# Frequencies to tokens on TensorE: the stationary operand takes all 128 channels in place of 64

## The chip, the cores and the metric

The kernel runs on one core of a Trainium2 chip. The metric is device time in microseconds (us) of one execution. TensorE (PE in the profile) multiplies: a load (PEld) puts the stationary operand into its array, a matmul streams the moving operand past it into a PSUM bank. VectorE (DVE), ScalarE (ACT) and GpSimdE (POOL) do elementwise work, and SyncE (SP) issues the DMA transfers.

## The reference

Two sequences of 3008 tokens with 256 channels are convolved with a filter through a Fourier transform over the tokens, and the tokens go through two multilayer perceptrons one after the other.

```python
def _attn_ref(x, filt_r, filt_i) -> np.ndarray:
    X = np.fft.rfft(x, axis=1)
    F = (filt_r + 1j * filt_i)[None, :, :]
    y = np.fft.irfft(X * F, n=x.shape[1], axis=1)
    return y.astype(np.float32)

def _moe_ref(x, w_gate, w_val, w_out):
    g = x @ w_gate
    silu = g * (1.0 / (1.0 + np.exp(-g)))
    return (silu * (x @ w_val) @ w_out).astype(np.float32)

def _moe2_ref(x, w_in, w_out):
    h = x @ w_in
    relu6 = np.clip(h + 3.0, 0.0, 6.0)
    return ((h * relu6 / 6.0) @ w_out).astype(np.float32)
```

The hidden widths are 1536 and 2048; the weights come in as 64-bit floats, which the kernel decodes itself.

## The kernel before

The transform over 3008 = 47 x 64 points is done as a transform over 47 and one over 64, both as matmuls with small matrices of sines and cosines that lie in the tile `mat`. Going forward, `over_n1` (L335) and `over_n2` (L351) make 24 x 64 frequencies, `filter_product` multiplies by the filter, and `back` (L377) undoes the transform over 64. The result goes to DRAM (`d2`) with the 24 frequencies, real and imaginary, in 48 rows. What is left is the transform back over 47 points: 48 rows of frequencies become 47 tokens. That is **`to_time`** (L157), the function that is changed.

`to_time` works in *turns*. One turn takes the frequencies `g[..., t - t0]` of 128 channels as the stationary operand and up to 47 columns of `mat` as the moving one, so that the 128 channels come out on the partitions of a PSUM bank and the tokens along its columns. A turn is done for r = 0 (rows 0 to 47 of the tiles, bank `accs[0]`) and for r = 1 (rows 64 to 111, bank `accs[1]`): these use the upper and the lower half of the rows of TensorE's array. Before, the 128 channels are also cut into two halves of 64 (`o` = 0 and 64), each with its own half of the array's columns: four matmuls a turn on the four quarters of the array. All operands are full f32.

It is called in three places:

- `form(0)`, at the end of the transform's loop (k = 16), and `form(1)`, in the first step (t = 0) of the first perceptron: 12 turns each, half of them for channels 0 to 127 (a = 0), half for 128 to 255 (a = 1). `form_end` splits the result into a high and a low part (L122 on ACT, L115 on DVE) as the operand `xs` of the perceptron's matmuls (L236, L244).
- `block_to_time`, twice (a = 0 and 1) for each of the token blocks 1 to 5: at t = 19 and 20 for block 1, and by `turn_x` at the place `T` of a unit for blocks 2 to 5. `evacuate` (L545 on ACT, L546 on DVE) copies the two banks away.

Blocks have 1024 tokens, two halves of 512; 512 columns are 12 turns (the first and the last turn are narrower), and the last block of 896 tokens has 10. So there are 12 + 12 + 2 x (4 x 12 + 10) = 140 turns, 560 matmuls before.

After the transform the program is a list of *units*, each one slice of 128 (first perceptron) or 256 (second) hidden columns for one block, written out by hand in the order in which every engine takes it: matmuls of L661 and L706 with f32r operands, 128x128 stationary and up to 512 moving columns. The planner `plan_x` puts `turn_x` for the next block two and one places ahead of its first use.

Of the kernel before, what the change touches and what calls it, by code (L numbers as in the profile page):

```python
# [16 lines left out]
P = 128  # L17
B, S, D = 2, 3008, 256
N1, N2 = 47, 64
N1P = 48  # L20
# [36 lines left out]
M1, CO, SI, NS, FIN, NM = 0, 48, 112, 176, 240, 288  # L57
# [20 lines left out]
def fft_conv_glu_mlp(ctx: ExitStack, tc: tile.TileContext, x, filt, mats, sgn, w1, w2, out):  # L78
    nc = tc.nc
# [9 lines left out]
    mat = keep.tile([P, NM], F32, name="mat")  # L89
# [35 lines left out]
    def rows(i, n=64):  # L125

        return slice(i * 64, i * 64 + n)
# [4 lines left out]
    def turns(first, n):  # L132

        return 32 * first // N1, -(-(32 * first + n // 2) // N1)
# [14 lines left out]
    def to_time(g, first, n, accs, a, at=0):  # L149

        t0, t1 = turns(first, n)
        lo, hi = 32 * first, 32 * first + n // 2
        for t in range(t0, t1):
            i0, i1 = max(lo, t * N1), min(hi, (t + 1) * N1)
            for o in range(0, P, 64):
                for r in range(2):
                    nc.tensor.matmul(accs[r][o:o + 64, at + i0 - lo:at + i1 - lo],  # L157
                                     g[rows(r, N1P), t - t0, o:o + 64],
                                     mat[rows(r, N1P), FIN + i0 - t * N1:FIN + i1 - t * N1])

    def block_to_time(g, block, accs, a):
        t, at = 0, 0
        for _, first, n in block:
            t0, t1 = turns(first, n * N2)
            to_time(g[:, t:t + t1 - t0], first, n * N2, accs, a, at)
            t, at = t + t1 - t0, at + n * N2 // 2
# [103 lines left out]
    with tc.manual_schedule():  # L270
# [176 lines left out]
        def form(j):  # L447
            if j == 0:
                xsd["both"] = new_xs()
            xsd[j] = xsd["both"][:, j * 2048:(j + 1) * 2048].rearrange("p (v k n) -> p v k n", v=2, k=2)  # L450
            accs = [bank("a"), bank("a")]
            for a in range(2):
                to_time(gt[j][a], FIRST[j][0], 512, accs, a, 256 * a)
            return accs
# [112 lines left out]
        for t in range(2 * plain):  # L567
# [55 lines left out]
            if 10 < t < 23:  # L623
                q, r = divmod(t - 11, 2)
# [351 lines left out]
```

## Time and profile before

| | |
|---|---|
| median of 3 runs | 1122.61 us (1122.2 to 1125.9) |
| the profiled execution: time | 1122.33 us |
| its span from first to last instruction | 1120.3 us |
| granted clock of TensorE, mean | 1.0 |
| busy share: matmuls, weight loads | 99%, 83% |
| busy share: DVE, ACT, POOL | 76%, 67%, 54% |

Matmuls are pipelined and overlap, so the busy share of the matmuls says that some matmul was in the array, not how fast they follow each other. For that, one reads how far apart the starts of loads or matmuls lie. A record's own duration is longer than that distance. In the views below a run of equal instructions is one row: its start, the time from the first start to the last end, and how many there are. Shapes such as `48*64 48x47` read: stationary operand of 48 rows and 64 columns, moving operand of 48 rows and 47 columns.

### The profile page before, as it was taken

Reading aid. Unit: us, or ns where it says so; the run is one execution under the profiler, and the core shown is the slowest. Engines: PE = TensorE matmul, PEld = TensorE weight load, DVE = VectorE, ACT = ScalarE, POOL = GpSimd, SP = SyncE. Lnnn points to the kernel's source line nnn. Section 1 sums busy time; section 2 is a strip of 40 time slices with the busy share of each in tenths; the row PEclk is TensorE's granted clock in tenths of the full one; section 3 lists DMA queues with packets and bytes.
Section 4 is the critical chain, followed back from the end, with each engine's and each line's share of the span. In section 5 each row is a group of like instructions: output and inputs, shape, how many; then the busy total and the mean of one; then the engine's idle time right before and its main releaser. Section 6 shows DMA issues by size and latency. Waiting matters only on the chain.

```text
span 1120.3 us, 19185 instructions
## 1 busy us (share of the span) xinstructions
PE 1109.2 (99%) x7246; PEld 924.5 (83%) x7246; DVE 856.1 (76%) x1164; ACT 751.8 (67%) x1363; POOL 605.0 (54%) x779
## 2 busy tenths in 40 slices
PE   9989999999999999999999999999999999999998
PEld 7768888888888888888899888888888888888997
DVE  4979977878878887786888877667677677677765
ACT  4554546667667767766767777777777677677764
POOL 4742366696765585574577645335435444354440
PEclk9999999999999999999999999999999999999999
DMA  9974954843733463272353421422322312412300
GB/s 315 284 204 144 265 203 144 233 154 122 196 124 121 141 177 104 83 202 80 116 199 125 165 82 70 153 77 65 142 78 78 138 68 78 148 52 77 116 27 33
DMA packets 58844, 150.75 MB, mean 135 GB/s; under 512 B 5568, under 2 KB 26016, under 8 KB 56992
## 3 DMA queue, kind: packets, MB, share of 16 engines
q1 hardware_dynamic: 58208, 149.01, 41.7%
q8 instruction: 56, 0.92, 0.3%
q10 hardware_dynamic: 544, 0.52, 0.1%
q14 instruction: 36, 0.29, 0.1%
HBM read 117.27 MB, written 32.24 MB: 133 GB/s over the span
## 4 chain that ended last, share of the span: by engine, by line
PE 95%; DVE 2%; POOL 1%; DMA 1%; ACT 1%; issue 0%; ACTq 0%; POOLq 0%; DVEq 0%
PE gv L661 45%; PE a L706 37%; PE gv L236 5%; PE a L244 2%; PE gv L377 1%; PE a L351 1%; PE gv L157 1%; PE gv L335 1%; POOL h L115 1%; DVE h L364 0%; DMA ring<-x_in 0%; DVE xs L115 0%; POOL h L118 0%; DMA w1f<-x 0%; DVE h L600 0%
## 5 line engine op out<-in xcount | busy, mean ns | idle before, releaser
L661 PE MATMUL gv<-xs,wu 128*128 128x512 f32 (+1 forms) x2268 | 566.8, 386 | 0.6 <-DVE h L600 0.6
L115 POOL TENSOR_TENSOR wu<-st,wu 128x224 fp32r<-128x224 f32 x432 | 312.7, 756 | 394.5 <-ACT wu L516 394.5
L661 PEld LDWEIGHTS gv<-xs,wu 128*128 128x128 f32 x2268 | 423.7, 188 | 81.6 <-ACT raw L545 1.7
L706 PE MATMUL a<-hs,wo 128*128 128x512 f32 (+1 forms) x1872 | 476.7, 385 | 0.0
L706 PEld LDWEIGHTS a<-hs,wo 128*128 128x128 f32 x1872 | 351.4, 188 | 65.4 <-ACT hs L694 0.3
L115 DVE TENSOR_TENSOR hs<-h,hs 128x512 fp32r<-128x512 f32 (+3 forms) x228 | 234.6, 1029 | 67.4 <-ACT hs L694 62.8
L694 ACT CAST hs<-h 128x512 fp32r<-128x512 f32 (+3 forms) x216 | 172.6, 799 | 126.7 <-DVE h L690 73.9
L115 POOL TENSOR_TENSOR wo<-st,wo 128x256 fp32r<-128x256 f32 x156 | 149.8, 973 | 0.0
L690 DVE SCALAR_TENSOR_TENSOR h<-h,gv 128x512 f32<-128x512 f32 (+1 forms) x144 | 96.5, 670 | 22.8 <-ACT h L684 22.6
L516 ACT CAST wu<-st 128x384 fp32r<-128x384 f32 x216 | 110.6, 563 | 0.4 <-DMA st<-w1f 0.4
L682 ACT ACTIVATE h<-gv 128x512 f32<-128x512 f32 (+1 forms) x120 | 70.7, 589 | 59.2 <-PE gv L661 57.8
L118 DVE TENSOR_TENSOR gv<-gv,h 128x512 f32<-128x512 f32 (+1 forms) x108 | 74.0, 685 | 41.9 <-PE gv L661 35.3
L684 ACT ACTIVATE h<-gv 128x512 f32<-128x512 f32 (+1 forms) x144 | 84.1, 584 | 15.4 <-PE gv L661 15.3
L871 ACT COPY gv<-gv 128x512 f32<-128x512 f32 (+1 forms) x108 | 60.9, 564 | 42.4 <-PE gv L661 38.6
L118 DVE TENSOR_TENSOR h<-gv,h 128x512 f32<-128x512 f32 (+1 forms) x108 | 73.0, 676 | 18.7 <-PE gv L661 18.3
L690 DVE SCALAR_TENSOR_TENSOR h<-h,h 128x512 f32<-128x512 f32 (+1 forms) x48 | 32.7, 681 | 58.7 <-ACT h L684 58.6
L875 ACT COPY h<-gv 128x512 f32<-128x512 f32 (+1 forms) x108 | 62.5, 579 | 16.4 <-PE gv L661 13.3
L688 DVE TENSOR_TENSOR h<-h 128x512 f32<-128x512 f32 (+1 forms) x60 | 61.6, 1027 | 1.8 <-ACT h L682 1.2
L115 DVE TENSOR_TENSOR xs<-raw,xs 128x512 fp32r<-128x512 f32 (+1 forms) x77 | 57.4, 747 | 0.1
L516 ACT CAST wo<-st 128x256 fp32r<-128x256 f32 (+1 forms) x108 | 54.1, 501 | 0.0
L559 ACT CAST xs<-raw 128x512 fp32r<-128x512 f32 (+1 forms) x77 | 45.7, 609 | 3.0 <-DVE raw L115 2.8
L236 PE MATMUL gv<-xs,wall_a 128*128 128x512 f32 x192 | 45.8, 392 | 0.1
(88 smaller groups left out, 898.1 us busy)
## 6 DMA issues: line engine op xcount, KB each, us to landing
st<-w1f SPq DMA_DIRECT2D x60, 576.0 KB, 3.9
st<-w2f SPq DMA_DIRECT2D x48, 704.0 KB, 4.2
raw<-w_in SPq DMA_DIRECT2D x16, 512.0 KB, 4.6
ring<-x_in SPq DMA_DIRECT2D x30, 256.0 KB, 5.3
x<-w_in SPq DMA_DIRECT2D x9, 768.0 KB, 5.3
d<-turned SPq DMA_DIRECT2D x32, 192.0 KB, 5.2
yd<-y SPq DMA_DIRECT2D x5, 1024.0 KB, 6.6
raw<-yd SPq DMA_DIRECT2D x5, 1024.0 KB, 7.1
```

Of the source, the lines that this page charges most:

```text
L115: (engine or nc.vector).tensor_tensor(out=out, in0=a, in1=b, op=ALU.subtract)
L118: (engine or nc.vector).tensor_tensor(out=out, in0=a, in1=b, op=ALU.add)
L236: nc.tensor.matmul(acc, w[:, r, c[k]:c[k] + P], xs[:, v, k], start=(r, v, k) == (0, 0, 0), stop=(r, k) == (1, 1))
L516: nc.scalar.copy(out=to[:, 0, at:at + hi - lo], in_=src[:, lo:hi])
L661: nc.tensor.matmul(acc[:, :n], w[:, r, FORM[a] * P:(FORM[a] + 1) * P], xs_part(k, v, i), start=start and q == 0, stop=q == 2, skip_group_c ...
L682: nc.scalar.activation(out=self.value(t, 0), in_=src, func=AF.Silu)
L684: nc.scalar.activation(out=self.value(t, a), in_=src, func=AF.Relu, bias=3.0)
L688: nc.vector.tensor_tensor(out=self.value(t, 0), in0=self.value(t, 0), in1=src, op=ALU.mult)
L690: nc.vector.scalar_tensor_tensor(out=self.value(t, a), in0=self.value(t, a), scalar=6.0, in1=src, op0=ALU.min, op1=ALU.mult)
L694: nc.scalar.copy(out=self.hs[:, t, :, 0, :self.n], in_=self.value(t))
L706: yield lambda t=t, v=v, a=a, j=j, r=r: nc.tensor.matmul(banks["a"][2 * j + t][:, :n], self.wo[:, r, (2 * a + j) * P:(2 * a + j + 1) * P], ...
L875: nc.scalar.copy(out=u.s7, in_=b3[:, :n])
```

## The change

The loop over the two halves of the channels goes, and the stationary operand of a matmul takes all 128 channels. A turn then has two matmuls, one on the upper and one on the lower half of the array's rows, each over all of its columns, instead of four. What is multiplied and where it is written stay the same.

```diff
             i0, i1 = max(lo, t * N1), min(hi, (t + 1) * N1)
-            for o in range(0, P, 64):
-                for r in range(2):
-                    nc.tensor.matmul(accs[r][o:o + 64, at + i0 - lo:at + i1 - lo],
-                                     g[rows(r, N1P), t - t0, o:o + 64],
-                                     mat[rows(r, N1P), FIN + i0 - t * N1:FIN + i1 - t * N1])
+            for r in range(2):
+                nc.tensor.matmul(accs[r][:, at + i0 - lo:at + i1 - lo], g[rows(r, N1P), t - t0],
+                                 mat[rows(r, N1P), FIN + i0 - t * N1:FIN + i1 - t * N1])
```

On TensorE, at the start of a burst for the third block (in the middle of the units; `gv0` and `gv1` are its two banks, and a row gives the partitions and columns that are written), the first two turns stand so before:

```order
L706 MATMUL a3_114<-hs_2641,wo_2526 128x512
L157 MATMUL gv0_107<-mat_69,g_2369 64x10
L157 MATMUL gv1_108<-mat_69,g_2369 64x10
L157 MATMUL gv0_107<-mat_69,g_2369 64x10
L157 MATMUL gv1_108<-mat_69,g_2369 64x10
L157 MATMUL gv0_107<-mat_69,g_2369 64x47
L157 MATMUL gv1_108<-mat_69,g_2369 64x47
L157 MATMUL gv0_107<-mat_69,g_2369 64x47
L157 MATMUL gv1_108<-mat_69,g_2369 64x47
```

and so in the changed kernel, whose lines have lower numbers by one here and by two further down:

```order
L704 MATMUL a3_114<-hs_2545,wo_2430 128x512
L156 MATMUL gv0_107<-mat_69,g_2273 128x10
L156 MATMUL gv1_108<-mat_69,g_2273 128x10
L156 MATMUL gv0_107<-mat_69,g_2273 128x47
L156 MATMUL gv1_108<-mat_69,g_2273 128x47
```

The two matmuls on channels 64 to 127 of each turn are gone, and the ones that stay write 128 partitions. Nothing else moves: the instruction ahead of the burst is the same.

The other place is where `form(0)` ends and `back(15)` begins, on TensorE too, between the transform and the first perceptron. Before, the last turn (21 columns) and the first matmuls behind it, which also work on quarters of the array, are these:

```order
L157 MATMUL a0_111<-mat_69,g_1016 64x21
L157 MATMUL a1_112<-mat_69,g_1016 64x21
L157 MATMUL a0_111<-mat_69,g_1016 64x21
L157 MATMUL a1_112<-mat_69,g_1016 64x21
L377 MATMUL gv3_110<-h_1234,mat_69 64x384
L377 MATMUL gv0_107<-h_1234,mat_69 64x384
```

In the changed kernel:

```order
L156 MATMUL a0_111<-mat_69,g_1016 128x47
L156 MATMUL a1_112<-mat_69,g_1016 128x47
L156 MATMUL a0_111<-mat_69,g_1016 128x21
L156 MATMUL a1_112<-mat_69,g_1016 128x21
L375 MATMUL gv3_110<-h_1234,mat_69 64x384
L375 MATMUL gv0_107<-h_1234,mat_69 64x384
```

Here the matmuls ahead of `back(15)` now use the array in halves, and those of `back(15)` still in quarters.

## Rows read from the trace of the kernel before

**Rows 1.** The page's first part: busy time, share of the span, instructions.
```profile
span 1120.3 us, 19185 instructions
PE 1109.2 (99%) x7246; PEld 924.5 (83%) x7246; DVE 856.1 (76%) x1164; ACT 751.8 (67%) x1363; POOL 605.0 (54%) x779
```

**Rows 2.** The page's chain that ended last: shares by engine, then by line.
```profile
PE 95%; DVE 2%; POOL 1%; DMA 1%; ACT 1%; issue 0%; ACTq 0%; POOLq 0%; DVEq 0%
PE gv L661 45%; PE a L706 37%; PE gv L236 5%; PE a L244 2%; PE gv L377 1%; PE a L351 1%; PE gv L157 1%; PE gv L335 1%; POOL h L115 1%; DVE h L364 0%; DMA ring<-x_in 0%; DVE xs L115 0%; POOL h L118 0%; DMA w1f<-x 0%; DVE h L600 0%
```

**Rows 3.** Busy time by stretch: length, PE, PEld, DVE, ACT, POOL, clock, DMA.
```profile
84.00:1119.00 1035.00, 1031.54 (x5476) 865.53 (x5474) 796.01 (x1065) 707.42 (x1252) 557.35 (x709) 1.00 0.39 124
```

**Rows 4.** Line L157: durations in ns (least/median/most), first and last start, shapes.
```profile
L157 PEld LDWEIGHTS gv<-mat,g x928: 129/135/135, 154.1 to 519.9; 48*64 48x64 f32 x186
...
L157 PEld LDWEIGHTS a<-mat,g x96: 129/135/136, 68.6 to 73.5; 48*64 48x64 f32 x96
...
L157 PEld LDWEIGHTS a<-mat,y x48: 129/135/135, 78.3 to 78.9; 48*64 48x64 f32 x48
...
L157 PEld LDWEIGHTS a<-mat,turned x48: 135/135/135, 79.0 to 79.6; 48*64 48x64 f32 x48
```

**Rows 5.** Timeline of TensorE's weight loads around two block bursts.
```profile
229.36 1.49 PEld L157 LDWEIGHTS gv<-mat,g 48*64 48x64 f32 x96 [0.35 <-issue]
230.90 0.19 PEld L661 LDWEIGHTS gv<-xs,wu 128*128 128x128 f32 x1
...
509.74 1.26 PEld L157 LDWEIGHTS gv<-mat,g 48*64 48x64 f32 x80 [0.35 <-issue]
```

**Rows 6.** Weight-load timeline, the last loads before a wait in `form(0)`.
```profile
69.98 0.20 PEld L157 LDWEIGHTS a<-mat,g 48*64 48x64 f32 x4
...
70.04 0.14 PEld L157 LDWEIGHTS a<-mat,g 48*64 48x64 f32 x2
```

**Rows 7.** Weight-load timeline of `over_n2`: quarters, 384 moving columns.
```profile
10.77 0.14 PEld L351 LDWEIGHTS a<-g,mat 64*64 64x64 f32 x4 [0.18 <-issue]
11.09 0.14 PEld L351 LDWEIGHTS a<-g,mat 64*64 64x64 f32 x4 [0.18 <-issue]
11.41 0.14 PEld L351 LDWEIGHTS a<-g,mat 64*64 64x64 f32 x4 [0.18 <-issue]
```

**Rows 8.** Loads of 128 columns: line L244, then two behind a burst (timeline).
```profile
L244 PEld LDWEIGHTS a<-hs,wall_b x48: 186/188/189, 155.6 to 183.9; 128*128 128x128 f32 x48
...
155.62 0.30 PEld L244 LDWEIGHTS a<-hs,wall_b 128*128 128x128 f32 x2
```

**Rows 9.** Loads of the opening stretch: groups (mean ns), then their timeline.
```profile
L320 PEld LDWEIGHTS gv<-turned 128*128 128x128 f32 x16 | 3.5, 330 | 1.1 <-DVE turned L314 1.1
L335 PEld LDWEIGHTS gv<-mat,ring 48*64 48x64 f32 x32 | 0.9, 218 | 0.2 <-issue 0.2
...
1.05 3.49 PEld L320 LDWEIGHTS gv<-turned 128*128 128x128 f32 x16 [1.05 <-DVE turned L314]
4.76 0.95 PEld L335 LDWEIGHTS gv<-mat,ring 48*64 48x64 f32 x32 [0.22 <-issue]
```

**Rows 10.** Timeline of TensorE's matmuls from `form(0)` to behind `form(1)`.
```profile
69.46 0.83 PE L157 MATMUL a<-mat,g 48*64 48x47 f32 x40
72.09 0.31 PE L157 MATMUL a<-mat,g 48*64 48x47 f32 x2 [1.80 <-DMA g<-d]
72.90 0.83 PE L157 MATMUL a<-mat,g 48*64 48x47 f32 x43 [0.50 <-DMA g<-d]
...
78.28 0.91 PE L157 MATMUL a<-mat,y 48*64 48x26 f32 x48
79.01 0.89 PE L157 MATMUL a<-mat,turned 48*64 48x26 f32 x48
79.83 4.47 PE L236 MATMUL gv<-xs,wall_a 128*128 128x512 f32 x16
```

**Rows 11.** Weight-load timeline where the perceptron first reads the second half's `xs`.
```profile
83.56 0.76 PEld L236 LDWEIGHTS gv<-xs,wall_a 128*128 128x128 f32 x4 [0.54 <-DVE xs L115]
```

## Prediction

> **What bounds the kernel now.** I first read the page's busy shares: TensorE's matmuls cover 99% of a span of 1120.3 us, and VectorE, the next busiest compute engine, 76% [rows 1]. The chain that ended last says the same more sharply: 95% of it is TensorE, and the changed line, L157, stands in it with 1% [rows 2]. Then I asked by stretch: from 84 us to the end, matmuls are busy in 1031.54 of 1035.00 us, at a granted clock of 1.00 [rows 3]. So whatever the order of the program puts on TensorE between 84 us and the end, longer or shorter, moves the end by as much; the other engines have slack. The change touches TensorE alone, so the question is how long a burst of turns lasts. Here the reader must not go by busy time, but by the distance of starts.
>
> **How a burst is paced now.** Line L157 has 928 + 96 + 48 + 48 = 1120 weight loads of 48x64, each with one matmul [rows 4]. The program has 560 matmuls there, so an f32 matmul goes through the array in two passes, and each pass loads its weights anew. A turn has four matmuls on four quarters; as these run side by side, I count in *rounds*: four loads, one for each quarter, and four matmuls. That makes 1120 / 4 = 280 rounds, two a turn.
>
> A burst of 96 loads (24 rounds) lasts 1.49 us from the first load's start to the last one's end [rows 5]; less the last load's own 0.135 us [rows 4] that is 1.355 us for 23 distances, **59 ns a round**. The burst of 80 gives (1.26 - 0.135) / 19 = 59 ns [rows 5].
>
> What sets the 59 ns? There are three candidates. First, the matmul: with 384 moving columns the rounds on quarters are 0.32 us apart (10.77, 11.09, 11.41) [rows 7], which is 0.83 ns a column; 47 columns would need 39 ns, too little. Second, issuing eight instructions: when the first half of `form(0)` runs out, only two quarters have work left, and the pairs of loads still start at 69.98 and 70.04 [rows 6], 0.06 us apart with half as many instructions. So it isn't the number of instructions. Third, the load of 64 columns. Its price shows in the step from 64 to 128 columns: the records last 135 ns [rows 4] and 188 ns [rows 8], 53 ns for 64 columns more. A round of 59 ns is then a load of 53 ns and some 6 ns around it, with the matmul of 39 ns running beside the next load. This is the reading that I take.
>
> **The change, part by part.** It removes 560 loads and 560 matmul passes, and the 560 loads that stay are of 128 columns. The two halves of the array have their own rows and their own banks, so I take it that they still run side by side. A turn keeps its two rounds; a round now has two loads of 128 columns beside each other. If the load paces, the round becomes 59 + 53 = **112 ns**.
>
> The trace has no 48x128 load with f32, so I bound the step from both sides. Low: where two loads of 128 columns follow each other with nothing between (155.62, two in 0.30 us, less 0.188), they start 0.11 us apart [rows 8]; that gives 110 - 59 = 51 ns a round. High: in the opening stretch everything on TensorE is slower, but the ratio can be read: 16 full-array f32 passes start (3.49 - 0.33) / 15 = 211 ns apart, and 8 rounds on quarters (0.95 - 0.218) / 7 = 105 ns [rows 9]; twice as long for twice the columns, which here would be 118 ns, 59 more. I take 53, which is a difference of two durations of the same kind at the same clock.
>
> The sum:
>
> - *Ten block bursts*, eight of 24 rounds and two of 20: 232 rounds, all in the stretch where TensorE has no slack [rows 3]. 232 x 53 ns = **+12.3 us**. Behind a burst, `evacuate` waits as before; ACT and DVE get the banks later by as much as TensorE goes on later.
> - *`form(1)`*, 24 rounds, lies between matmuls of L236 without a wait of TensorE [rows 10]: **+1.3 us**.
> - *`form(0)`*: its first 12 rounds end ahead of a wait of 1.80 us for the load of `g` [rows 10] and their 0.6 us disappear in it. The other 12 rounds start when the load lands, and `form_end` and the first L236 wait for them: 12 x 53 ns = **+0.6 us**.
> - *A wait that shrinks*: at 83.56 TensorE's loads wait 0.54 us for DVE's low part of the second half [rows 11]. `form(1)` lasting longer delays TensorE's first step more than DVE's queue, which is busy until then with other work, so some of this is given back: between 0 and 0.5, I take **-0.3 us**.
> - *Change between quarters and halves of the array*: between `form(0)` and `back(15)` both were on quarters. A burst that starts behind full-array work shows 0.35 us without a load [rows 5], most of it the last matmul still streaming. I take **+0.1 us**, from a range of 0 to 0.35. At the other 11 bursts the array changes its division before and after as it did.
>
> Together +12.3 + 1.3 + 0.6 - 0.3 + 0.1 = **+14.0 us**. The profiled execution took 1122.33 us (span 1120.3 and 2.0 around it), so its counterpart takes 1136.3; the median of the runs lies 0.3 above the profiled one, which gives **1136.6 us**, 1.2% slower.
>
> The fewer matmul passes give nothing back, because they were not what paced a round; nothing else leans on TensorE's instruction count.
>
> **The rivals.**
>
> *Nothing changes.* The 59 ns could be a fixed price of any pass, whatever it loads and streams. For it: the 39 ns of the matmul do not explain the round, and the 59 ns hold in bursts with different mixes of narrow turns [rows 5]. Against it: two 128-column loads stood 110 ns apart [rows 8]. It decides if a 128-column load on half the array takes under 59 ns. The time would be 1122.6 (0.1 for `back(15)` is below what can be seen). The Trainium skill, TensorEngine Tiling (Array Packing), section Instruction Overhead, has such a rule: a matmul has an overhead of about 60 cycles, so that one moving column takes as long as sixty. By that rule alone the number of stationary columns would not count at all, and the sum would be nothing; the 110 ns between wide loads speak against leaving the load out.
>
> *Faster.* Issue paces a round after all: 8 instructions in 59 ns become 4 in 29.5, and 268 rounds (280 less the 12 hidden) give -7.9 us, 1114.7. The rows with two quarters at work, still 60 ns apart [rows 6], speak against it, and so do the wide loads [rows 8]. It decides only if a wide load takes less than 59 ns and a round has no floor.
>
> *Load and matmul in series.* With two matmuls in flight instead of four, each half could load, then stream: 59 + 53 + 39 = 151 ns a round, +92 ns; 268 x 92 ns = 24.7, with -0.2 for the last two terms 1147.1. Against it: the quarters with 384 columns are paced by the matmul alone [rows 7], so a quarter loads while it streams.
>
> *The halves' loads in series.* If two wide loads could not go side by side, a round would take 2 x 110 = 220 ns, +161 ns; 268 x 161 ns = 43.1, with the same -0.2 1165.5. Against it: four narrow ones do.
>
> **How the numbers follow.** Load-paced 0.77; in series with the matmul 0.06; the halves in series 0.06; nothing 0.06; faster 0.05. The likeliest's own range: low, 51 ns a round on 268 rounds less 0.5, +13.2, 1135.8; high, 59 ns, nothing given back, 0.35 for the change of division and 0.1 more at each of 11 bursts, +17.3, 1139.9. To leave out no more than 2 in 10 the range goes from 1134 (a little under the low end, for the runs' scatter) to 1148, which takes in the load and matmul in series: 0.77 + 0.06 = 0.83. Under 0.3%, 3.4 us, a measurement of this kernel cannot be told from no change: faster 0.05, same 0.06, slower 0.77 + 0.06 + 0.06 = 0.89.
>
> **What the changed profile would show.** 560 loads of 48x128 at L156, each near 188 ns, and block bursts of 48 loads in (23 x 112 + 188) ns = 2.76 us instead of 1.49: this is the step on which all hangs. The pairs of loads start 112 ns apart; at 59 the fixed price is right, near 150 the series, over 200 the halves exclude each other. The share of L157's successor in the chain doubles to some 2 or 3%. The wait at 83.56 is shorter or gone, the wait of 1.80 us in `form(0)` is shorter by 0.6, and no new wait of TensorE for `raw` shows. The prediction is wrong if a round isn't paced by its load, or if a change between halves and whole or quarters costs other than one between quarters and whole: 11 bursts have two each.

## The result and the profile after

The changed kernel takes 1138.6 us (median of four runs, 1134.84 to 1140.79) against 1122.93 for the kernel before on the same chip: a ratio of 1.0136, 95% interval 1.0116 to 1.0156. The forecast of 1136.6 us lies 2.0 below the median and, as a ratio of 1.0125, inside the interval. Executions that took over 1.5% longer than the fastest of their kernel are left out of every median here: one of the kernel before, one of the forms alone, and the profiled one of the changed kernel's repeat.

The page of the changed kernel, first part, and two lines of its chain that ended last:

```profile
span 1135.1 us, 18065 instructions
PE 1125.8 (99%) x6686; PEld 939.2 (83%) x6686; DVE 853.2 (75%) x1164; ACT 752.4 (66%) x1363; POOL 597.4 (53%) x779
...
PE 96%; DMA 1%; SPq 1%; DVE 1%; POOL 0%; ACT 0%; issue 0%; ACTq 0%; POOLq 0%
PE gv L659 45%; PE a L704 37%; PE gv L234 5%; PE a L242 2%; PE gv L156 2%; PE gv L375 1%; PE a L349 1%; PE gv L333 1%; SPq L384 1%; DMA ring<-x_in 0%; PE a L156 0%; DMA d<-turned 0%; DMA g<-d 0%; POOL h L115 0%; SPq L441 0%
```

Beside [rows 1, 2]: 560 loads and 560 matmuls fewer (6686 for 7246), and yet the matmuls' busy time has risen by 16.6 us and the span by 14.8. The other engines have as much work as before. The block bursts (now L156) have gone from 1% to 2% of the chain.

The same bursts as in [rows 5] and the loads' durations, in the timeline of the weight loads and the view of line L156 (durations least/median/most):

```profile
232.54 2.76 PEld L156 LDWEIGHTS gv<-mat,g 48*128 48x128 f32 x48 [0.35 <-issue]
235.34 0.30 PEld L659 LDWEIGHTS gv<-xs,wu 128*128 128x128 f32 x2
...
521.94 2.31 PEld L156 LDWEIGHTS gv<-mat,g 48*128 48x128 f32 x40 [0.35 <-DMA st<-w1f]
...
L156 PEld LDWEIGHTS gv<-mat,g x464: 182/188/188, 155.1 to 534.1; 48*128 48x128 f32 x155
```

A burst of 24 rounds takes 2.76 us where it took 1.49, one of 20 rounds 2.31 where it took 1.26. A round takes (2.76 - 0.188) / 23 = 112 ns instead of 59. The ten block bursts all show this growth, 8 x 1.27 + 2 x 1.05 = 12.3 us.

One thing in this trace stood in no step of the forecast. The stretches of the changed kernel (length; busy time of PE, PEld, DVE, ACT, POOL; granted clock; DMA share and GB/s) and, from the kernel before, the stretch behind its corresponding burst:

```profile
232.50:235.30 2.80, 2.80 (x49) 2.76 (x48) 0.01 (x1) 0.62 (x1) 2.72 (x6) 1.00 0.73 267
236.20:239.60 3.40, 3.40 (x10) 2.63 (x10) 2.16 (x2) 1.77 (x4) 3.40 (x5) 0.50 0.49 150
240.00:244.00 4.00, 4.00 (x20) 3.24 (x19) 2.26 (x3) 1.93 (x5) 3.61 (x6) 1.00 0.28 108
...
72.40:75.80 3.40, 3.40 (x23) 1.38 (x21) 2.55 (x4) 1.09 (x3) 0.00 (x0) 0.50 0.67 273
```
```profile
232.20:235.60 3.40, 3.40 (x16) 2.77 (x15) 1.77 (x3) 1.97 (x4) 3.40 (x5) 1.00 0.43 115
```

Behind the burst of 232.54 the granted clock is 0.50 for 3.4 us, the lower of the two levels (1.2 instead of 2.4 GHz), and so it is behind `form(0)`. The one behind `form(0)` is no part of the change: it also stands in two kernels below whose `form(0)` is the one of before (half of the channels, and 32 columns for half of the channels; their stretches follow), and not in one whose `form(0)` is changed (falling order).

```profile
74.70:78.10 3.40, 3.40 (x19) 1.74 (x11) 2.99 (x4) 1.73 (x4) 0.00 (x0) 0.50 0.69 282
...
74.30:77.70 3.40, 3.40 (x35) 1.79 (x28) 2.38 (x4) 1.44 (x3) 0.00 (x0) 0.50 0.79 311
```

In the 3.4 us behind the burst 10 matmuls touch the window, where before it is 16: at 0.23 us each that is 1.4 us lost. The mean granted clock of the four runs is 0.992 to 0.998, so the number of such stretches differs from run to run, and the shortest run has the highest clock.

### The profile page after: what moved, and what is told of

Same layout as the page of the kernel before. It is cut to its first block, busy times and chain, and to the rows that moved or that the text cites. A ratio compares the mean times of both kernels' runs of the same rounds, so it can differ in the third digit from the quotient of the medians.

```text
span 1135.1 us, 18065 instructions
## 1 busy us (share of the span) xinstructions
PE 1125.8 (99%) x6686; PEld 939.2 (83%) x6686; DVE 853.2 (75%) x1164; ACT 752.4 (66%) x1363; POOL 597.4 (53%) x779
## 4 chain that ended last, share of the span: by engine, by line
PE 96%; DMA 1%; SPq 1%; DVE 1%; POOL 0%; ACT 0%; issue 0%; ACTq 0%; POOLq 0%
PE gv L659 45%; PE a L704 37%; PE gv L234 5%; PE a L242 2%; PE gv L156 2%; PE gv L375 1%; PE a L349 1%; PE gv L333 1%; SPq L384 1%; DMA ring<-x_in 0%; PE a L156 0%; DMA d<-turned 0%; DMA g<-d 0%; POOL h L115 0%; SPq L441 0%
## 5 line engine op out<-in xcount | busy, mean ns | idle before, releaser
L115 POOL TENSOR_TENSOR wu<-st,wu 128x224 fp32r<-128x224 f32 x432 | 308.4, 745 | 414.6 <-ACT wu L514 414.6
```

Source lines behind the costliest of these rows:

```text
L115: (engine or nc.vector).tensor_tensor(out=out, in0=a, in1=b, op=ALU.subtract)
```

## The experiments

The theory: a round is paced by the weight load, whose time goes by the number of stationary columns; quarters or halves of the array work side by side, and the matmul runs beside the next load. Its rivals: a fixed price for each pass; the instructions handed out; something shared between quarters or halves. A second question came up with the result: whether the stretches at 0.50 behind block bursts belong to the change. In the cuts, `wide` is the number of stationary columns and `upto` the channel at which the loop stops; `form(0)` and `form(1)` are called with 64 columns and all channels where they stay as before.

**Half of the channels, two operands.** In the block bursts:

```diff
-            for o in range(0, P, 64):
+            for o in range(0, upto, wide):
...
+            to_time(g[:, t:t + t1 - t0], first, n * N2, accs, a, at, 64, 64)
```

> Forms as before; in the ten block bursts only channels 0 to 63 of each 128 are formed (the others are left out, so the output isn't the reference's): two matmuls a turn as in the changed kernel, but of 64 stationary columns. If the columns of the load pace a round, it stays at 59 ns and the time at that of the kernel before (within 0.5 us). If it is having two operands in flight instead of four that costs, the rounds go to 112 ns and the time to about +12 us.

Timeline of its loads at the third block:

```profile
230.75 1.48 PEld L157 LDWEIGHTS gv<-mat,g 48*64 48x64 f32 x48 [0.35 <-issue]
```

48 loads take the time of 96 before: rounds of (1.48 - 0.135) / 23 = 58 ns with two loads in each instead of four. The ratio to the kernel before is 0.9993 (0.9977 to 1.0010). Neither the number of operands in flight nor that of instructions paces a round at 59 ns.

**One half of the array.** In the block bursts, with 128 stationary columns:

```diff
-            for o in range(0, P, 64):
-                for r in range(2):
...
+            for o in range(0, P, wide):
+                for r in range(2 if wide < P else 1):
```

> Forms as before; in the ten block bursts only the matmuls of r = 0 are made, with 128 stationary columns (half of the tokens are left out, so the output isn't the reference's). If the two halves of the array load side by side, one half alone keeps rounds of 112 ns and costs +12 us against before, as both do. If the halves share the path of the weights, rounds fall to about 56 ns and the time is that of before.

```profile
232.80 2.75 PEld L157 LDWEIGHTS gv<-mat,g 48*128 48x128 f32 x24 [0.35 <-issue]
```

In this timeline 24 loads take as long as 48 in the changed kernel: 111 ns each with the other half idle. So the halves do not share the path of the weights. The time is 1.0119 of the kernel before (1.0091 to 1.0147), as costly as twice the work, though a larger part of it comes from stretches at 0.50 (the table further down).

**The other direction: 32 columns.** First with all channels, eight matmuls a turn in all twelve bursts:

```diff
-            for o in range(0, P, 64):
+            for o in range(0, P, 32):
...
-                    nc.tensor.matmul(accs[r][o:o + 64, at + i0 - lo:at + i1 - lo],
-                                     g[rows(r, N1P), t - t0, o:o + 64],
+                    nc.tensor.matmul(accs[r][o:o + 32, at + i0 - lo:at + i1 - lo],
+                                     g[rows(r, N1P), t - t0, o:o + 32],
```

> The opposite direction: a turn has eight matmuls on eighths of the array (48x32 stationary operands) instead of four on quarters. If the weight load paces a round, 32 columns load in some 27 + 6 = 33 ns, the matmul of 47 columns (39 ns and a little around it) takes over, and a round takes about 42 ns: 268 rounds x -17 ns = -4.5 us against the kernel before. If a round is a fixed price of 59 ns, or if 16 instructions a round take longer to hand out than the load, nothing or less is won: loads of different quarters stood 6.6 ns apart where they were free to go, and 8 x 6.6 = 53 ns would give -1.6 us.

This missed by far: 1145.13 us, a ratio of 1.0193 (1.0167 to 1.0219). A burst without a pause, one with a pause, and the pages' lines for one queue that carries instructions, in this kernel and in the kernel before:

```profile
253.84 1.76 PEld L157 LDWEIGHTS gv<-mat,g 48*32 48x32 f32 x192 [0.35 <-issue]
...
238.82 1.73 PEld L157 LDWEIGHTS gv<-mat,g 48*32 48x32 f32 x189 [0.35 <-issue]
243.03 0.18 PEld L157 LDWEIGHTS gv<-mat,g 48*32 48x32 f32 x3 [2.47 <-issue]
...
q8 instruction: 65, 1.06, 0.4%
...
q8 instruction: 56, 0.92, 0.3%
```

With all eight operands a round takes (1.76 - 0.106) / 23 = 72 ns, more than the 59 of four quarters. Over 268 rounds that is +3.5 us. On top, TensorE stops for 1.9 to 2.5 us inside five of the ten block bursts, 11.3 us in all, and the profile names no cause; stretches at 0.50 come with the pauses (the table further down). The queue shows 65 packets of 16 KB where it was 56, so it carries more when TensorE has more instructions. The table has the start of the packet that falls nearest to each pause, to 0.1 us below:

| burst from | pause of the loads from | to | packet starts |
|---|---|---|---|
| 167.10 | 168.56 | 170.86 | 168.2 |
| 238.82 | 240.55 | 243.03 | 240.6 |
| 338.19 | 339.82 | 341.99 | 339.6 |
| 435.61 | 437.13 | 438.98 | 436.6 |
| 534.45 | 535.88 | 538.36 | 535.9 |

Every pause ends 2.4 to 2.7 us after a packet has started in the middle of the burst; in the five bursts without a pause no packet starts before the last 0.3 us. So it is likely that the pauses wait for instructions; that is read from the order in time, and no run gave TensorE its instructions sooner.

To tell the columns from the rest, the same with four operands of 32 columns, for half of the channels in the block bursts (forms as before):

```diff
-            for o in range(0, P, 64):
+            for o in range(0, upto, wide):
...
+            to_time(g[:, t:t + t1 - t0], first, n * N2, accs, a, at, 32, 64)
```

> Forms as before; in the block bursts four matmuls a turn on eighths of the array, with 32 stationary columns each, for channels 0 to 63 of each 128 (the others are left out, so the output isn't the reference's). With eight eighths a round took 67 to 72 ns. If handing out 16 instructions a round was what took that time, 8 of them are out of the way here: the load of 32 columns (33 ns) and the matmul of 47 (42 ns) are left, rounds of about 42 ns, bursts of 24 rounds near 1.1 us and -3.9 us against before. If stationary operands of 32 columns are slow in themselves, rounds stay near 70 ns and it costs +2.5 us.

```profile
230.66 1.05 PEld L157 LDWEIGHTS gv<-mat,g 48*32 48x32 f32 x96 [0.35 <-issue]
...
L157 PEld LDWEIGHTS gv<-mat,g x928: 102/109/119, 155.6 to 518.1; 48*32 48x32 f32 x186
```

96 loads, as many as before the change, in 1.05 us instead of 1.49 [rows 5]: (1.05 - 0.109) / 23 = 41 ns a round, where 42 were expected from the matmul of 47 columns. The ratio is 0.9967 (0.9952 to 0.9982), -3.7 us where -3.9 were expected. So a fixed price of 59 ns falls too: the round follows the columns of the load, 112 ns at 128 and 59 at 64, and at 32 columns, where the matmul of 47 columns is expected to take over, it is 41. The loss with eight operands does not come with the 32 columns. Whether it comes with 16 instructions a round or with eight operands in flight, this run cannot tell: it halves both.

**Forms alone, blocks alone.** The width is handed to `to_time` as a parameter, 128 in one kind of call and 64 in the other:

```diff
+                to_time(gt[j][a], FIRST[j][0], 512, accs, a, 256 * a, 64)   (blocks alone)
+            to_time(g[:, t:t + t1 - t0], first, n * N2, accs, a, at, 64)     (forms alone)
```

> Wide stationary operands (128 channels) in form(0) and form(1) alone, the block bursts on quarters as before. By the prediction's terms +1.3 and +0.6 - 0.3 + 0.1 = +1.7 us against before. If instead most of the change sits in the turn from halves to quarters at back(15), it is well over 3 us; if form(0) and form(1) hide behind the loads of g and the queue of VectorE, it is nothing.

The ratio is 1.0013 (0.9999 to 1.0028), +1.5 us by its middle, where +1.7 were expected; the interval reaches down to nothing. Its matmul timeline from `form(0)` on:

```profile
71.86 0.42 PE L157 MATMUL a<-mat,g 48*128 48x47 f32 x2 [1.06 <-DMA g<-d]
72.76 1.51 PE L157 MATMUL a<-mat,g 48*128 48x47 f32 x22 [0.48 <-DMA g<-d]
74.21 2.47 PE L377 MATMUL gv<-h,mat 64*64 64x384 f32 x16
76.61 3.68 PE L236 MATMUL gv<-xs,wall_a 128*128 128x512 f32 x12
80.22 1.54 PE L157 MATMUL a<-mat,y 48*128 48x26 f32 x24
81.58 1.52 PE L157 MATMUL a<-mat,turned 48*128 48x26 f32 x24
83.02 7.34 PE L236 MATMUL gv<-xs,wall_a 128*128 128x512 f32 x31
```

The wait for `g` is 1.06 us where it was 1.80 [rows 10], and `form(1)` lasts from 80.22 to 83.02 instead of from 78.28 to 79.83: 2.80 us for 1.55, +1.25 as summed.

> Wide stationary operands in the ten block bursts alone, the forms on quarters as before. By the prediction 232 rounds x 53 ns = +12.3 us, and something more where the granted clock falls behind a burst, some 1.7 us for each stretch of 3.4 us at 0.50. If bursts were partly hidden by slack of TensorE behind them (evacuation that ends later anyway), less than 12.

```profile
232.23 2.76 PEld L157 LDWEIGHTS gv<-mat,g 48*128 48x128 f32 x48 [0.35 <-issue]
```

The ratio is 1.0092 (1.0067 to 1.0117), +10.3 us with +7.5 to +13.1; its bursts of 24 rounds last 2.76 us. The two parts together make +11.8 by their middles, the whole change 1.0136 and 1.0124 in its two measurements. The ten block bursts are nearly all of it. Well over 3 us in the change of division at `back(15)` is excluded by the interval of the forms alone, which ends at +3.1 us; a few tenths would not show.

**Is the clock part of the change?** Turns in falling order, and each matmul streams up to 64 columns more, into columns that later turns overwrite:

```diff
-        for t in range(t0, t1):
+        for t in reversed(range(t0, t1)):
             i0, i1 = max(lo, t * N1), min(hi, (t + 1) * N1)
+            w = min(64, i0 - lo)
             for r in range(2):
-                nc.tensor.matmul(accs[r][:, at + i0 - lo:at + i1 - lo], g[rows(r, N1P), t - t0],
-                                 mat[rows(r, N1P), FIN + i0 - t * N1:FIN + i1 - t * N1])
+                nc.tensor.matmul(accs[r][:, at + i0 - w - lo:at + i1 - lo], g[rows(r, N1P), t - t0],
+                                 mat[rows(r, N1P), FIN + i0 - w - t * N1:FIN + i1 - t * N1])
```

> The changed kernel with turns in falling order, each matmul after the first turn of a segment streaming 64 columns more, whose results the next turns overwrite: up to 111 moving columns, 93 ns by 0.83 ns a column. If the load alone paces a round and the matmul runs beside it, rounds stay at 112 ns and bursts at 2.76 us. If load and matmul share the time, a round grows by 53 ns and the kernel by 14 us. The changed kernel showed a granted clock of 0.50 for 3.4 us behind some bursts, other ones in each run, and its runs scatter over 6 us: if that comes of the array standing idle for much of each round, here the clock stays at 1.00 and the time lies at 1133 to 1135 with little scatter; if it comes of anything else, the stretches at 0.50 stay and the time is that of the changed kernel, 1135 to 1141.

Its loads, its shapes (the most frequent has 111 moving columns), and the stretch that held a fall in the changed kernel:

```profile
232.35 2.76 PEld L157 LDWEIGHTS gv<-mat,g 48*128 48x128 f32 x48 [0.35 <-issue]
...
L157 PE MATMUL gv<-mat,g x464: 232/272/359, 154.7 to 532.3; 48*128 48x111 f32 x109, 48*128 48x57 f32 x4, 48*128 48x91 f32 x4, 48*128 48x109 f32 x4
...
230.00:250.00 20.00, 20.00 (x159) 16.70 (x158) 11.60 (x16) 10.41 (x20) 18.20 (x28) 1.00 0.49 154
```

A burst with 111 moving columns lasts 2.76 us, to the digit that of the changed kernel with 47: the matmul hides behind the load. The mean granted clock of the profiled execution is 1.000. The median is 1135.22 us (1132.40 to 1137.72), a ratio of 1.0100 (1.0078 to 1.0122).

Then once more, on one chip with the changed kernel:

> The changed kernel once more, beside the others on one chip: 1135 to 1141 us, with stretches at a granted clock of 0.50 behind some bursts, and a mean granted clock of 0.992 to 0.998 in its runs. If the stretches at 0.50 of the first profile were chance, they are gone here.

> The wide moving operand once more on the same chip as the changed kernel. If the matmul's extra columns are hidden behind the load, and keep the clock up, this is 2 to 4 us faster than the changed kernel, with no stretch at 0.50 behind a block burst; if the difference between the two was chance, they tie.

The changed kernel took 1139.62 us (median of five runs, 1135.02 to 1141.56; clocks 0.993 to 0.998), 1.0124 of the kernel before (1.0099 to 1.0150); there is no trace of these five, so their stretches cannot be counted. The one with wide moving operands took 1135.19 (1133.93 to 1137.96; clocks 0.996 to 1.000), 1.0098 (1.0077 to 1.0120). It was expected to be 2 to 4 us faster; it was by 4.4 between the medians and by 2.9 between the means, and the two intervals overlap. As the order of the turns also differs, the order alone:

```diff
-        for t in range(t0, t1):
+        for t in reversed(range(t0, t1)):
```

> The control for the wide moving operand: the changed kernel with its turns in falling order, and nothing else. If the extra columns kept the clock up, and not the order, this is as the changed kernel: 1135 to 1141 us, mean granted clock 0.993 to 0.998, stretches at 0.50 behind block bursts. If the order did it, it is as the wide one: around 1135, clock 0.996 to 1.000.

It took 1140.70 us (1134.64 to 1142.51; clocks 0.994 to 0.998), like the changed kernel. Its loads at the third block, and the stretch behind the burst:

```profile
248.31 2.76 PEld L156 LDWEIGHTS gv<-mat,g 48*128 48x128 f32 x48 [0.35 <-issue]
...
252.00:255.40 3.40, 3.40 (x10) 2.63 (x10) 2.99 (x3) 1.83 (x4) 3.40 (x4) 0.50 0.45 170
```

What settles it is the count of stretches at 0.50 in the traces, read in windows of 0.4 us over each whole span (without the last microseconds, where the program has ended):

| kernel | stationary / moving columns in the block bursts | in or behind block bursts | behind `form(0)` |
|---|---|---|---|
| before | 64 / 47 | 0 | 0 |
| half of the channels | 64 / 47 | 0 | 1 |
| 32 columns, half of the channels | 32 / 47 | 0 | 1 |
| forms alone | 64 / 47 | 0 | 1 |
| wide moving operand, first trace | 128 / 111 | 0 | 0 |
| wide moving operand, second trace | 128 / 111 | 0 | 1, of 6.8 us |
| changed | 128 / 47 | 1 | 1 |
| blocks alone | 128 / 47 | 3 | 0 |
| falling order | 128 / 47 | 3 | 0 |
| one half of the array | 128 / 47 | 5, two of them of 6.8 us | 0 |
| 32 columns, all channels | 32 / 47 | 5, each in or behind a pause | 1, of 6.8 us |

Apart from the kernel with pauses, stretches at 0.50 stand with block bursts only where rounds took 112 ns and 47 columns streamed in each, and in neither trace of the kernel that streams 111 beside the same loads.

## Why the prediction was right

*What bounds it.* Right in the main: TensorE stayed the chain that ended last (96%), and the bursts' growth reached the end. Two waits gave a little back. The first stands in no step of the forecast, which took it that from 84 us on TensorE has no slack: a wait for VectorE in the first block's units, before and in the changed kernel, is 0.37 us shorter.

```profile
177.35 0.76 PEld L661 LDWEIGHTS gv<-xs,wu 128*128 128x128 f32 x4 [0.83 <-DVE h L600]
...
180.64 1.00 PEld L659 LDWEIGHTS gv<-xs,wu 128*128 128x128 f32 x5 [0.46 <-DVE h L598]
```

The second is the forecast's own shrinking wait, which gave back 0.6 and not 0.3 (below).

*A round is paced by its load, 59 + 53 = 112 ns.* Right, as closely as rows at two decimals can show, and shown by experiment rather than argued: 41, 59 and 112 ns for 32, 64 and 128 columns, the same with two operands as with four at 64, the same with one half of the array as with two at 128. The Trainium skill, TensorE: Matmul & The Clock Gate, section LDWEIGHTS (loading the stationary operand), says that a load's time goes by its columns and not by its rows, at 1.2 columns a nanosecond. The trace agrees: 53 ns for 64 columns more. One of the forecast's two bounds does not carry, though: the 211 ns between passes of the opening [rows 9] need not be the load, since those matmuls (L320, `128*128 128x128`) stream 128 columns each; it set only the upper end of the range.

*Halves side by side, and matmul beside load.* Right: one half alone keeps 111 ns, and 111 moving columns instead of 47 change nothing. Both rivals "in series" fall with that, and the faster one and the fixed price with the experiments on 64 and 32 columns. The rule that the prediction takes from the Trainium skill, TensorEngine Tiling (Array Packing), section Instruction Overhead, some 60 cycles for each matmul, does not decide here: with the same 47 moving columns the rounds take 41, 59 and 112 ns.

*The terms.* Ten block bursts +12.3: 12.3 by the bursts' lengths. `form(1)` +1.3: 1.25. `form(0)` cannot be read in one execution, since the load of `g` lands up to 1.8 us earlier or later from run to run (71.86 and 70.31 in two kernels with the same transfers); forms alone measure +1.5 where the terms give +1.7. The shrinking wait, -0.3: the wait of 0.54 us at 83.56 [rows 11] is gone, and so is one of 0.29 us ahead of it that the forecast did not name.

```profile
82.72 0.30 PEld L236 LDWEIGHTS gv<-xs,wall_a 128*128 128x128 f32 x2 [0.29 <-ACT xs L122]
...
81.45 6.70 PEld L234 LDWEIGHTS gv<-xs,wall_a 128*128 128x128 f32 x30
```

Right behind `form(1)` TensorE's loads start 1.63 us later than before (81.45 for 79.82), and the one that started at 83.56 starts at 84.56, only 1.00 us later: 0.6 given back.

*What the sum lacked, and some luck.* The stretches at 0.50 behind block bursts stand in no term. Their price shows in the stretch from the first perceptron's first matmul to the end of the span, here for the kernel before, the wide moving operand, the changed kernel and the falling order:

```profile
75.05 3.31 PE L236 MATMUL gv<-xs,wall_a 128*128 128x512 f32 x12
...
75.27 3.05 PE L235 MATMUL gv<-xs,wall_a 128*128 128x512 f32 x12
...
75.66 3.06 PE L234 MATMUL gv<-xs,wall_a 128*128 128x512 f32 x12
...
77.42 3.16 PE L234 MATMUL gv<-xs,wall_a 128*128 128x512 f32 x12
```

With spans of 1120.3, 1133.2, 1135.1 and 1140.3 us that is 1045.3, 1057.9, 1059.4 and 1062.9: +12.7, +14.2 and +17.6 against before, with none, one and three such stretches, so some 1.5 us each, close to the 1.4 above. The sum's terms for this part, 12.3 + 1.3 - 0.3 = +13.3, are 0.6 above the +12.7 without such stretches; waits that shrink or grow by a few tenths, the two above among them, lie in that difference. Ahead of the first perceptron one execution differs from another by more than the forecast's terms there: with the same `form(0)` as before, its first matmul starts at 72.58 in the trace of blocks alone and at 77.23 in that of 32 columns and half of the channels.

By medians the wide kernel is +11.2 and +11.0 us over the kernel before (intervals some 2.5 us either way), and the changed kernel +15.3 and +13.9; the sum was +14.0. So the forecast is close for its mechanism, and to within 2 us also because stretches that it did not know of made up for terms that, by the wide kernel's medians, came out below the sum. Where the rest of that shortfall lies is not shown.

## What to carry to other kernels

With small f32 matmuls that load new weights each time, count rounds and ask what paces one: the load by its stationary columns, the matmul by its moving columns, or, perhaps, the instructions. Merging matmuls along the stationary columns halves the instructions and here nearly doubled the round (59 to 112 ns), so it loses where loads of neighbouring column groups run side by side and pace the rounds. Fewer instructions are worth something only where rows show that they pace; with four operands a round they did not, and with eight it is likely, not shown.

## What the runs showed of the hardware that was not expected

The granted clock fell to 0.50 in or behind bursts in which rounds followed each other 112 ns apart and 47 columns streamed in each. In the 8 us ahead of each of these stretches (changed kernel, blocks alone, falling order, one half of the array) TensorE's matmuls show no pause of 0.1 us, and its weight loads none over the 0.35 us that stand ahead of a burst in the kernel before too [rows 5]. The Trainium skill, TensorE: Matmul & The Clock Gate, section HAM oscillation, tells of falls through waits between groups of matmuls; here falls came without one. The kernel that streamed 64 useless columns more beside the same loads had none behind its block bursts in two traces, and took 1.0100 and 1.0098 of the time before, where the changed kernel and its falling order took 1.0124 to 1.0141. With eight small operands a round, TensorE paused 1.9 to 2.5 us inside half of the bursts; each pause ended 2.4 to 2.7 us after a packet of instructions had started, and why stays open.
